# Second products of an MLP moved between attention scores, in row tiling

## The chip, the cores and the metric

The kernel runs on one core of a Trainium2 chip. The metric is the device time of one execution in microseconds. Most executions agree within 0.3%; times below are medians of several runs. A ratio between two kernels is the mean time of one kernel's fast runs over the mean of the other's of the same rounds, so it is not quite the ratio of the medians quoted beside it. Where two kernels are said to differ by so many us, that is the difference of their ratios, taken of 430 us.

## The reference

Attention with one extra unit in the softmax denominator, then an MLP with a squared ReLU:

```python
# q, k, v: (8, 12, 448, 64); w_in: 768 x 2048; w_out: 2048 x 768
scores = q @ k.T / sqrt(64);  e = exp(scores - m)
attn = e / (sum(e) + exp(-m) + 1e-9)
x = (attn @ v)                 # as 3584 tokens x 768
r = maximum(x @ w_in, 0)       # "first product"
out = (r * r) @ w_out          # "second product", float32
```

## The kernel before

The program is a loop over 54 units. A unit is a pair of heads of one batch (batch 0 is cut in two, so it has 12 units; from unit 12 on a unit covers all 448 queries). A unit computes its scores and exponentials, and row sums and values of the unit before it. After unit 53 one more pass does row sums and values alone; where a text speaks of the last unit, which has no scores, it means this pass. MLP work of earlier batches is poured in between, so that TensorE (the matrix engine) always has something to do while ScalarE exponentiates.

TensorE can be split into tiles. Scores contract over 64 numbers, so two of them run at once in two halves of the rows (row tiling). Values and row sums have 64 outputs, so two run at once in halves of the columns (column tiling). MLP products fill the array (full tiling), or are written as two column halves when they follow the values. All of them write the banks of PSUM, eight in this kernel, which the other engines then read ("evict"). In the code `drain` issues MLP matmuls; in the texts a drain is the pause of TensorE at a change of tiling.

```python
s_psum = ... bufs=2 (two banks each)   x_psum = ... bufs=1   m_psum = ... bufs=3   # 8 banks

def product(out_, lhsT, rhs, start, stop):
    if halved[0]:
        for x in (0, 64):
            nc.tensor.matmul(out_[x:x + 64], lhsT[:, x:x + 64], rhs, start=start, stop=stop)
    else:
        nc.tensor.matmul(out_, lhsT, rhs, start=start, stop=stop)

# the loop, shortened
    scores(u, et, 0)
    drain(share[0] * 0.45)             # MLP matmuls, full tiling
    scores(u, et, 1)
    rcp = row_sums(prev, pes)
    values(prev, pet, xp, 0); values(prev, pet, xp, 1)
    halved[0] = True
    drain(share[0] * 0.15)             # MLP matmuls, column halves
    for step in range(3):
        add_chunks(u, et, es, step)    # VectorE: three additions for the next row sums
        drain(share[0] * (0.15, 0.1, 0.15)[step])
    normalise(prev, xp, rcp)           # VectorE: values * reciprocal of row sums
```

A first-product tile is taken from PSUM by VectorE (relu, then square); a second-product tile by ScalarE (copy with a scale).

The softmax here doesn't subtract the row's maximum and nothing guards it: scores larger than these inputs give would overflow.

## Time and profile before

| | before |
|---|---|
| time, median of runs | 430.2 us |
| span of the profiled run | 430.7 us |
| TensorE, VectorE, ScalarE busy | 98%, 57%, 57% |
| chain of work that ended last (followed back from the last instruction), on TensorE | 92% |

The page gives busy time of each engine, but a busy TensorE is not one at its peak. What counts is the distance between starts of consecutive matmuls, compared with the columns that they stream. The prediction below reads that. One caution on this profile: the profiled execution itself took 432.5 us, 2 us over the median. Its clock records are at half rate from 11.6 to 18.4 us, which no later profile here has, and unit 13 starts at 47.04 us where the others have 44.8 to 45.6. So 2 us of its early part are chance.

### The profile page before, as it was taken

The page shows a single profiled execution, that of the slowest core. Times are in us where ns is not written, and L with a number is a line of the kernel's source. Part 1 is how long each engine was busy: PE and PEld are TensorE (multiplying, and loading weights), DVE is VectorE, ACT ScalarE, POOL GpSimd, SP SyncE. Part 2 cuts the span into 40 slices and gives each one's busy share as a digit, 9 for nine tenths or more (in the row PEclk, how much of TensorE's full clock was granted, in tenths as well). Part 3 has the DMA queues.
Part 4 walks back from the last instruction along what each step waited for, and adds up shares of the span by engine and source line. Part 5 has one row for each costly group of instructions (what it writes and reads, how often), then busy time and mean ns, then how long its engine had stood idle before and what let it go on. Part 6 is the DMA issues. An engine that isn't in the chain of part 4 may idle for free.

```text
span 430.7 us, 9136 instructions
## 1 busy us (share of the span) xinstructions
PE 421.4 (98%) x3975; PEld 248.1 (58%) x3975; DVE 246.6 (57%) x489; ACT 247.6 (57%) x359; POOL 33.2 (8%) x52
## 2 busy tenths in 40 slices
PE   8989899999999999999999999999999999999996
PEld 3557675554465666554556665654556666564454
DVE  4759695268822596348842488248762278428700
ACT  4698867764555756674456755774555655740011
POOL 7541100010000100010000100030000000000000
PEclk9699899999999999999999999999999999999999
DMA  9999999399312893259811697139902200010022
GB/s 200 197 197 204 209 218 180 96 156 210 58 39 75 146 215 63 74 83 214 128 37 52 99 223 127 39 61 207 192 3 75 74 3 2 37 54 22 0 75 74
DMA packets 79129, 47.56 MB, mean 110 GB/s; under 512 B 50672, under 2 KB 75120, under 8 KB 78704
## 3 DMA queue, kind: packets, MB, share of 16 engines
q0 software_dynamic: 24160, 22.17, 32.2%
q1 hardware_dynamic: 54208, 24.11, 25.5%
q10 hardware_dynamic: 720, 0.69, 0.6%
q8 instruction: 31, 0.51, 0.5%
q14 instruction: 10, 0.08, 0.1%
HBM read 45.71 MB, written 19.32 MB: 151 GB/s over the span
## 4 chain that ended last, share of the span: by engine, by line
PE 92%; DVE 2%; ACT 2%; DMA 2%; issue 1%; ACTq 0%
PE mp L254 37%; PE mp L252 31%; PE sp L187 9%; PE xp L223 8%; PE mp L231 3%; PE sp L175 2%; DMA kr<-in_k_dram 2%; ACT et L155 1%; PE mp L147 1%; PE mp L376 1%; DVE es L204 1%; DVE qk L150 0%; ACT rcp L233 0%; DVE xt L242 0%; DVE es L208 0%
## 5 line engine op out<-in xcount | busy, mean ns | idle before, releaser
L155 ACT ACTIVATE et<-sp 112x896 f16<-112x896 f32 (+2 forms) x192 | 165.9, 914 | 109.8 <-PE sp L187 92.1
L200 DVE TENSOR_TENSOR es<-et 112x896 f16<-112x896 f16 x84 | 51.6, 622 | 103.5 <-ACT et L155 103.4
L274 DVE TENSOR_SCALAR rt<-mp 128x512 f16<-128x512 f32 (+1 forms) x122 | 77.4, 635 | 35.3 <-PE mp L252 24.1
L254 PE MATMUL mp<-xt,win 128*128 128x512 f16 (+3 forms) x456 | 84.8, 339 | 0.0
L254 PE MATMUL mp<-wout,g 128*128 128x512 f16 (+1 forms) x471 | 82.3, 330 | 0.0
L252 PE MATMUL mp<-wout,g 128*64 128x256 f16 (+1 forms) x850 | 71.9, 322 | 0.0
L252 PE MATMUL mp<-xt,win 128*64 128x384 f16 (+3 forms) x816 | 71.2, 325 | 0.2 <-DVE xt L242 0.2
L254 PEld LDWEIGHTS <-g 128*128 128x128 f16 x471 | 44.3, 98 | 33.9 <-issue 2.5
L304 ACT ACTIVATE ot<-mp 128x512 f32<-128x512 f32 (+1 forms) x56 | 27.3, 487 | 63.4 <-PE mp L254 51.7
L254 PEld LDWEIGHTS <-win 128*128 128x128 f16 x456 | 41.6, 98 | 36.6 <-issue 2.1
L252 PEld LDWEIGHTS <-g 128*64 128x64 f16 x850 | 47.7, 110 | 19.4
L252 PEld LDWEIGHTS <-win 128*64 128x64 f16 x816 | 45.4, 110 | 22.6 <-issue 1.0
L276 DVE TENSOR_TENSOR g<-rt 128x512 f16<-128x512 f16 (+1 forms) x124 | 49.5, 399 | 6.5 <-ACT rt L272 2.3
L223 PE MATMUL xp<-et,vn 112*64 112x448 f16 (+2 forms) x432 | 46.5, 338 | 0.3 <-DVE xt L242 0.3
L187 PE MATMUL sp<-qk 64*112 64x224 f16 x576 | 42.8, 268 | 0.0
L187 PEld LDWEIGHTS <-qk 64*112 64x112 f16 x576 | 26.9, 128 | 25.4 <-issue 25.4
L233 ACT ACTIVATE rcp<-mp,one_b 128x448 f32<-128x448 f32 (+2 forms) x54 | 32.2, 597 | 3.1 <-PE mp L231 2.8
L242 DVE TENSOR_TENSOR xt<-xp,rcp 128x448 f16<-128x448 f32 (+2 forms) x54 | 30.6, 566 | 3.5 <-ACT rcp L234 3.5
L223 PEld LDWEIGHTS <-vn 112*64 112x64 f16 x432 | 24.8, 112 | 10.3 <-issue 0.6
L234 ACT ACTIVATE rcp<-rcp 128x448 f32<-128x448 f32 (+2 forms) x54 | 28.9, 535 | 1.7
L78 POOL DMA_DIRECT2D vn<-in_v_dram x10 | 9.0, 902 | 243.2 <-PE xp L223 229.1
L202 DVE TENSOR_TENSOR es<-es 112x896 f16<-112x896 f16 x42 | 26.1, 623 | 1.0
(36 smaller groups left out, 136.5 us busy)
## 6 DMA issues: line engine op xcount, KB each, us to landing
out_dram<-ot SPq DMA_DIRECT2D x11, 384.0 KB, 2.3
vn<-in_v_dram POOLq DMA_DIRECT2D x6, 672.0 KB, 9.1
stage_q<-in_q_dram POOLq DMA_DIRECT2D x5, 676.0 KB, 11.1
stage_k<-in_k_dram POOLq DMA_DIRECT2D x5, 676.0 KB, 14.0
win<-in_moe_w_in_dram POOLq DMA_DIRECT2D x8, 384.0 KB, 13.8
wout<-in_moe_w_out_dram POOLq DMA_DIRECT2D x4, 768.0 KB, 20.2
out_dram<-ot SPq DMA_DIRECT2D x8, 288.0 KB, 2.6
out_dram<-ot SPq DMA_DIRECT2D x8, 192.0 KB, 2.7
```

The costliest lines, as they stand in the source:

```text
L155: nc.scalar.activation(out=out_, in_=in_, func=AF.Exp, scale=scale)
L187: nc.tensor.matmul(sp[:, odd, h * (S // 2):(h + 1) * (S // 2)], qk[r, which, kx:kx + 2 * P - 1:2], qk[r, 0, x:x + S // 2], start=True, sto ...
L200: nc.vector.tensor_add(f[:, step], e[:, 2 * step], e[:, 2 * step + 1])
L223: nc.tensor.matmul(xp[64 * h:64 * h + 64, 0:n], vns[b][:, 2 * pr + h, kk, :], of_head(chunk(et, u, c, kk), u, h), start=(kk == 0), stop=(k ...
L233: nc.scalar.activation(out=rcp[:, 0:n], in_=zp[:, 0:n], func=AF.Ln, bias=one_b)
L234: nc.scalar.activation(out=rcp[:, 0:n], in_=rcp[:, 0:n], func=AF.Exp, scale=-1.0)
L242: nc.vector.tensor_mul(xts[b // 2][:, pr, c:c + n], xp[:, 0:n], rcp[:, 0:n])
L252: nc.tensor.matmul(out_[x:x + 64], lhsT[:, x:x + 64], rhs, start=start, stop=stop)
L254: nc.tensor.matmul(out_, lhsT, rhs, start=start, stop=stop)
L274: nc.vector.tensor_scalar(out=rt[:, 0:m], in0=hp[:, 0:m], scalar1=0.0, scalar2=None, op0=ALU.max)
L276: nc.vector.tensor_mul(g[:, 0:m], rt[:, 0:m], rt[:, 0:m])
L304: nc.scalar.activation(out=ot[:, n0:n1], in_=op[:, 0:n1 - n0], func=AF.Copy, scale=OUT_SCALE)
```

## The change

The intent is to save changes of tiling. Between a unit's two halves of scores, which run in row tiling, a second product now runs in row tiling too: the 2048 contracted numbers are taken as two halves of each block of 128, one per row tile, into two PSUM banks. ScalarE evicts the first bank and VectorE adds the second. After the values come first products, in column halves. Work is handed out in whole tiles, and second products of a batch wait one batch longer.

```diff
+    def tile_out(t0, ts, n0, n1):
+        ...
+        lo = m_psum.tile([128, 512], FP32, name="mp") if rows else None
+        for fb in range(NFFB):
+            g = gts[t0][fb][:, ts * 128:(ts + 1) * 128]
+            if rows:
+                for x, o in ((0, op), (64, lo)):
+                    nc.tensor.matmul(o[:, 0:w], g[x:x + 64], wout[x:x + 64, fb, n0:n1], ...)
+        ...
+        nc.scalar.activation(out=ot[:, n0:n1], in_=op[:, 0:w], func=AF.Copy, scale=OUT_SCALE)
+        if rows:
+            nc.vector.scalar_tensor_tensor(out=ot[:, n0:n1], in0=lo[:, 0:w], scalar=OUT_SCALE,
+                                           in1=ot[:, n0:n1], op0=ALU.mult, op1=ALU.add)
 ...
-             2 * NPAIR - 1: [(1, 128, 256), (2, 0, 128), (2, 128, 256)]}
+             2 * NPAIR - 1: [(1, 128, 256), (2, 0, 128)]}
+    last, t0 = (2, 128, 256), 384
 ...
-        ready[(b + 2) * NPAIR - 1] = [(1, t0, n), (2, t0, n)]
+        ready[(b + 2) * NPAIR - 1] = [(1, t0, n), last]      # second product of the batch before
+        last = (2, t0, n)
 ...
+    def later_batch(i, u, prev, xp, pet, pes):               # from unit 12 on
+        if u:
+            scores(u, et, 0)
+            if outs and i >= MIXED + 3:
+                mode[0] = ROWS2
+                budget -= run(outs)                          # one second-product tile, 512 or 256 wide
+            else: ...                                        # first products, full tiling
+            scores(u, et, 1)
+        rcp = row_sums(prev, pes)
+        values(...)
+        others = [three additions] if u else []
+        others.append(lambda: normalise(prev, xp, rcp))
+        mode[0] = COLS2
+        while True:
+            ...                                              # first products, or spare second ones
+            budget -= run(tiles)
+            if others:
+                others.pop(0)()
+        for o in others:
+            o()
```

More of the change, by code (lines that the diff above doesn't have):

```diff
@@ L242, in normalise @@
         nc.vector.tensor_mul(xts[b // 2][:, pr, c:c + n], xp[:, 0:n], rcp[:, 0:n])
-    gts = {}
-    halved = [False]
+    gts, ots = {}, {}
+    FULL, COLS2, ROWS2 = range(3)
+    mode = [FULL]
     def product(out_, lhsT, rhs, start, stop):
-        if halved[0]:
+        if mode[0] == COLS2:
             for x in (0, 64):
@@ L254, in product, with tile_in @@
             nc.tensor.matmul(out_, lhsT, rhs, start=start, stop=stop)
-    def mlp_in(t0, n):
-        gt = gts[t0] = []
+    def tile_in(t0, n, f0, per):
+        gt = gts.setdefault(t0, [])
         xt, x0 = xts[t0 // (2 * S)], t0 % (2 * S)
-        per = max(1, 512 // n) if n < 384 else 1
-        for f0 in range(0, NFFB, per):
-            hp = m_psum.tile([128, 512], FP32, name="mp")
-            for j in range(per):
-                fb = f0 + j
-                for dc in range(DCH):
-                    product(hp[:, j * n:(j + 1) * n], win[:, dc, fb * 128:(fb + 1) * 128],
-                            xt[:, dc, x0:x0 + n], start=(dc == 0), stop=(dc == DCH - 1))
-                    if j < per - 1 or dc < DCH - 1:
-                        yield n / 2.4
-            m = per * n
-            rt = r_pool.tile([128, 512], FP16, name="rt")
-            if t0 == 0 and f0 % 8 == 0:
-                nc.scalar.activation(out=rt[:, 0:m], in_=hp[:, 0:m], func=AF.Relu)
-            else:
-                nc.vector.tensor_scalar(out=rt[:, 0:m], in0=hp[:, 0:m], scalar1=0.0, scalar2=None, op0=ALU.max)
-            g = g_pool.tile([128, 512], FP16, name=f"g{f0}")
-            nc.vector.tensor_mul(g[:, 0:m], rt[:, 0:m], rt[:, 0:m])
-            for j in range(per):
-                gt.append(g[:, j * n:(j + 1) * n])
-            yield n / 2.4
+        hp = m_psum.tile([128, 512], FP32, name="mp")
+        for j in range(per):
+            fb = f0 + j
+            for dc in range(DCH):
+                product(hp[:, j * n:(j + 1) * n], win[:, dc, fb * 128:(fb + 1) * 128],
+                        xt[:, dc, x0:x0 + n], start=(dc == 0), stop=(dc == DCH - 1))
+                if j < per - 1 or dc < DCH - 1:
+                    yield n / 2.4
+        m = per * n
+        rt = r_pool.tile([128, 512], FP16, name="rt")
+        if t0 == 0 and f0 % 8 == 0:
+            nc.scalar.activation(out=rt[:, 0:m], in_=hp[:, 0:m], func=AF.Relu)
+        else:
+            nc.vector.tensor_scalar(out=rt[:, 0:m], in0=hp[:, 0:m], scalar1=0.0, scalar2=None, op0=ALU.max)
+        g = g_pool.tile([128, 512], FP16, name=f"g{f0}")
+        nc.vector.tensor_mul(g[:, 0:m], rt[:, 0:m], rt[:, 0:m])
+        for j in range(per):
+            gt.append(g[:, j * n:(j + 1) * n])
+        yield n / 2.4
     def store(c, ot, n0, n1):
@@ L291, in store @@
             c += m
-    def mlp_out(t0, n):
-        gt = gts.pop(t0)
-        for ts in range(n // 128):
-            ot = osb_pool.tile([128, DM], FP32, name="ot")
-            for n0, n1 in ((0, 512), (512, DM)):
-                op = m_psum.tile([128, 512], FP32, name="mp")
-                for fb in range(NFFB):
-                    product(op[:, 0:n1 - n0], gt[fb][:, ts * 128:(ts + 1) * 128], wout[:, fb, n0:n1],
-                            start=(fb == 0), stop=(fb == NFFB - 1))
-                    if fb < NFFB - 1:
-                        yield (n1 - n0) / 2.4
-                nc.scalar.activation(out=ot[:, n0:n1], in_=op[:, 0:n1 - n0], func=AF.Copy, scale=OUT_SCALE)
-                if n1 == DM or t0 + ts * 128 + 128 == NT:
-                    store(t0 + ts * 128, ot, 0 if n1 < DM or t0 + ts * 128 + 128 < NT else n0, n1)
-                if n1 < DM:
-                    yield (n1 - n0) / 2.4
-            yield (DM - 512) / 2.4
+    def tile_out(t0, ts, n0, n1):
+        w = n1 - n0
+        tok = t0 + ts * 128
+        if n0 == 0:
+            ots[tok] = osb_pool.tile([128, DM], FP32, name="ot")
+        ot = ots[tok]
+        op = m_psum.tile([128, 512], FP32, name="mp")
+        rows = mode[0] == ROWS2
+        lo = m_psum.tile([128, 512], FP32, name="mp") if rows else None
[3 more added lines that the diff above has]
+                for x, o in ((0, op), (64, lo)):
+                    nc.tensor.matmul(o[:, 0:w], g[x:x + 64], wout[x:x + 64, fb, n0:n1],
+                                     start=(fb == 0), stop=(fb == NFFB - 1))
+            else:
+                product(op[:, 0:w], g, wout[:, fb, n0:n1], start=(fb == 0), stop=(fb == NFFB - 1))
+            if fb < NFFB - 1:
+                yield w / 2.4
+        nc.scalar.activation(out=ot[:, n0:n1], in_=op[:, 0:w], func=AF.Copy, scale=OUT_SCALE)
+        if rows:
+            nc.vector.scalar_tensor_tensor(out=ot[:, n0:n1], in0=lo[:, 0:w], scalar=OUT_SCALE, in1=ot[:, n0:n1],
+                                           op0=ALU.mult, op1=ALU.add)
+        last = tok + 128 == NT
+        if n1 == DM or last:
+            store(tok, ot, n0 if last else 0, n1)
+        yield w / 2.4
     warm = consts.tile([128, 512], FP16)
@@ L336, with left, run @@
     load_v(1, 3, 6)
-    work, left = [], [0.0]
+    ins, outs, begun = [], [], []
     def queue(part, t0, n):
-        work.append((mlp_in if part == 1 else mlp_out)(t0, n))
-        left[0] += (NFFB * DCH * n if part == 1 else n // 128 * NFFB * DM) / 2.4
+        if part == 1:
+            per = max(1, 512 // n) if n < 384 else 1
+            for f0 in range(0, NFFB, per):
+                ins.append([per * DCH * n / 2.4, tile_in(t0, n, f0, per)])
+        else:
+            for ts in range(n // 128):
+                for n0, n1 in ((0, 512), (512, DM)):
+                    outs.append([NFFB * (n1 - n0) / 2.4, tile_out(t0, ts, n0, n1)])
+    def left():
+        return sum(t[0] for t in ins + outs)
+    def run(tiles):
+        ns, gen = tiles.pop(0)
+        for _ in gen:
+            pass
+        return ns
     def drain(ns):
-        while work and ns > 0:
-            got = next(work[0], None)
+        while ins and ns > 0:
+            got = next(ins[0][1], None)
             if got is None:
-                work.pop(0)
+                ins.pop(0)
             else:
                 ns -= got
-                left[0] -= got
+                ins[0][0] -= got
     FIRST = 192
@@ L357 @@
     NU = len(units)
-    ready = {NPAIR - 1: [(1, 0, 128)],
-             2 * NPAIR - 1: [(1, 128, 256), (2, 0, 128), (2, 128, 256)]}
-    t0 = 384
+    MIXED = 2 * NPAIR
+    ready = {NPAIR - 1: [(1, 0, 128)], 2 * NPAIR - 1: [(1, 128, 256), (2, 0, 128)]}
+    last, t0 = (2, 128, 256), 384
     for b in range(1, B):
         n = 384 if b % 2 == 0 else 512
-        ready[(b + 2) * NPAIR - 1] = [(1, t0, n), (2, t0, n)]
+        ready[(b + 2) * NPAIR - 1] = [(1, t0, n), last]
+        last = (2, t0, n)
         t0 += n
@@ L389, in take_up, with first_batch @@
                 queue(*part)
-            share[0] = left[0] / NPAIR
-    for i in range(NU + 1):
-        u = units[i] if i < NU else None
-        prev = units[i - 1] if i > 0 else None
-        xp = rcp = None
-        if prev:
-            pet, pes = et, es
-            xp = x_psum.tile([128, 512], FP32, name="xp")
-        if u:
-            b, pr = u[0:2]
-            if pr == 0 and 0 < b and b + 1 < B:
-                load_v(b + 1, 0, NPAIR)
-                stage(b + 1)
-            et = e_pool.tile([P, RUN * 2 * S], FP16, name="et")
-            es = e_pool.tile([P, 4 * S], FP16, name="es")
-            scores(u, et, 0)
-            if i == 0:
-                keep_warm(4)
-            elif i < NPAIR:
-                keep_warm(1)
-                scores(u, et, 1)
-            if i == NPAIR:
-                rcp = row_sums(prev, pes)
-                values(prev, pet, xp, 0)
-                values(prev, pet, xp, 1)
-                normalise(prev, xp, rcp)
-                take_up(i - 1)
-            if i in transpose_at:
-                transposes(*transpose_at[i])
-            if i in regroup_at and i < NPAIR:
-                regroup(*regroup_at[i])
-            drain(share[0] * (0.45 if i != NPAIR else 0.0))
-            if i == 0 or i >= NPAIR:
-                scores(u, et, 1)
+            share[0] = left() / NPAIR
+    def first_batch(i, u, prev, xp, pet, pes):
+        scores(u, et, 0)
+        if i == 0:
+            keep_warm(4)
+        elif i < NPAIR:
+            keep_warm(1)
+            scores(u, et, 1)
+        rcp = None
+        if i == NPAIR:
+            rcp = row_sums(prev, pes)
+            values(prev, pet, xp, 0)
+            values(prev, pet, xp, 1)
+            normalise(prev, xp, rcp)
+            take_up(i - 1)
+        if i in transpose_at:
+            transposes(*transpose_at[i])
+        if i in regroup_at and i < NPAIR:
+            regroup(*regroup_at[i])
+        if i > NPAIR:
+            drain(share[0] * 0.45)
+        if i == 0 or i >= NPAIR:
+            scores(u, et, 1)
         if prev and i != NPAIR:
@@ L432 @@
             regroup(*regroup_at[i])
-        halved[0] = u is not None
+        mode[0] = COLS2
         drain(share[0] * 0.15)
         for step in range(3):
-            if u:
-                add_chunks(u, et, es, step)
+            add_chunks(u, et, es, step)
             drain(share[0] * (0.15, 0.1, 0.15)[step])
-        halved[0] = False
+        mode[0] = FULL
         if prev and i != NPAIR:
             normalise(prev, xp, rcp)
+    def later_batch(i, u, prev, xp, pet, pes):
+        togo = NPAIR - (i - 1) % NPAIR
+        budget = left() / togo
+        if u:
+            scores(u, et, 0)
+            if i in transpose_at:
+                transposes(*transpose_at[i])
+            if outs and i >= MIXED + 3:
+                mode[0] = ROWS2
+                budget -= run(outs)
+                mode[0] = FULL
+            else:
+                ns = 0.0
+                while ins and ns < 1500.0 and ns + 0.5 * ins[0][0] < budget:
+                    ns += run(ins)
+                budget -= ns
+            scores(u, et, 1)
+        rcp = row_sums(prev, pes)
+        values(prev, pet, xp, 0)
+        values(prev, pet, xp, 1)
+        if i in regroup_at:
+            regroup(*regroup_at[i])
+        others = []
+        if u:
+            others += [lambda step=step: add_chunks(u, et, es, step) for step in range(3)]
+        others.append(lambda: normalise(prev, xp, rcp))
+        mode[0] = COLS2
+        while True:
+            tiles = outs if i >= MIXED + 3 and (len(outs) > togo - 1 or not ins) else ins
+            if not tiles or 0.5 * tiles[0][0] > budget:
+                break
+            budget -= run(tiles)
+            if others:
+                others.pop(0)()
+        mode[0] = FULL
+        for o in others:
+            o()
@@ new lines @@
+    for i in range(NU + 1):
+        u = units[i] if i < NU else None
+        prev = units[i - 1] if i > 0 else None
+        pet, pes = et, es
+        xp = x_psum.tile([128, 512], FP32, name="xp") if prev else None
+        if u:
+            b, pr = u[0:2]
+            if pr == 0 and 0 < b and b + 1 < B:
+                load_v(b + 1, 0, NPAIR)
+                stage(b + 1)
+            et = e_pool.tile([P, RUN * 2 * S], FP16, name="et")
+            es = e_pool.tile([P, 4 * S], FP16, name="es")
+        if i < MIXED:
+            first_batch(i, u, prev, xp, pet, pes)
+        else:
+            later_batch(i, u, prev, xp, pet, pes)
+        if i != NPAIR:
@@ L444 @@
             transposed_loads(b + 1)
-    drain(1e12)
+    queue(*last)
+    before = len(outs) - last[2] // 64
+    while ins or outs:
+        if outs and (not ins or before > 0 and before * NFFB >= len(ins) * 6):
+            run(outs)
+            before -= 1
+        else:
+            run(ins)
 _INS = ['q', 'k', 'v', 'moe_w_in', 'moe_w_out']
```

## The prediction

> **What bounds the kernel now.** I read the page first (busy shares, the chain that ended last), then the waits of TensorE, then TensorE's order of time in one steady pair, then the first 90 us, where transfers matter. The page says that TensorE is busy almost throughout, and that the chain that ended last runs through it for 92% of the span:
>
> ```profile
> PE 421.4 (98%) x3975; PEld 248.1 (58%) x3975; DVE 246.6 (57%) x489; ACT 247.6 (57%) x359; POOL 33.2 (8%) x52
> ...
> PE 92%; DVE 2%; ACT 2%; DMA 2%; issue 1%; ACTq 0%
> ```
>
> The waits view of TensorE lists seven waits, 5.8 us together; the two longest entries are below (total, times, longest), and all are in the first 50 us. So nothing in the steady part starves TensorE, and only what TensorE itself spends can be saved there.
>
> ```profile
> PE mp L231 <- DVE es L208: 2.2, 3, 1.0
> PE mp L376 <- DVE warm L313: 1.2, 1, 1.2
> ```
>
> Busy is not peak, though. In TensorE's order of time (start, duration, line), one pair is scores, 15 full products, scores, row sums, values, then products in column halves:
>
> ```profile
> 206.59 0.59 PE L187 MATMUL sp<-qk 64*112 64x224 f16 x8
> 207.12 3.41 PE L254 MATMUL mp<-xt,win 128*128 128x512 f16 x15
> 210.46 0.59 PE L187 MATMUL sp<-qk 64*112 64x224 f16 x8
> 210.98 0.38 PE L231 MATMUL mp<-es,ones 112*64 112x448 f16 x2
> 211.20 0.92 PE L223 MATMUL xp<-et,vn 112*64 112x448 f16 x8
> ```
>
> The reader is to look at distances of starts. Consecutive full products start 216 ns apart, but 15 of them take 210.46 - 207.12 = 3.34 us, 0.10 more than 15 x 0.216. Score matmuls run as two row tiles at once, a pair every 95 ns, yet four pairs take 0.53 us and not 0.38. The loss is at changes of tiling. I took the start of every matmul between 88 and 376 us and subtracted its streaming time (columns at 2.4 per ns). Inside one tiling the excess is 2 to 3 ns. At changes the medians are: row to full 98, first full product another 10; full to row 96, first row pair another 48; row to column 96 plus 26 at the first; column to row 99 plus 48. A pair has four changes, 252 ns for going to full and back, 269 ns for going to column and back.
>
> **What the Trainium skill says.** "TensorEngine Tiling (Array Packing)", section Key Properties: changing the tiling mode drains the TensorEngine, changing the tile does not. The trace agrees, with the 96 to 99 ns above. The same page, Gotcha 1, says that row tiles must write different PSUM banks; that is why the changed product takes two. The trace shows it for the scores, whose two row tiles write two banks and keep 95 ns per pair of 224 columns. "TensorE: Matmul & The Clock Gate", section "What's actually happening", says that an idle window of about 3.4 us halves TensorE's clock for at least such a window. This trace has clock records at half from 45.7 to 49.1 us, after waits of 0.72 and 0.41 us at 44 to 45 us, so a hole need not even be a whole window long.
>
> **The change part by part.**
> (1) Tiling. From unit 15 on (units counted in the program's loop, 54 in all), one second product, 512 or 256 columns wide, sits between the two score halves in row tiling. Row to full and back goes away: 252 ns. I worked the queue rule through by hand-count: 35 of units 15 to 53 get such a product; 17, 18, 23, 24 find no second product and use full first products. Two of the 35 (15, 16) lie in the early part, discussed under (4). 33 x 0.252 = 8.3 us saved. The change to column and back stays.
> (2) Streaming. A row-tiled product of 128x512 is two matmuls of 64 rows together, as a column-tiled one is two of 64 columns together. I take 216 ns per pair for 512 and 109 for 256, as in column and full tiling. The risk is the weights: two loads of 64x128 per pair. The scores do two loads of 64x112 per 95 ns; scaled to 128 columns, 109 ns (an estimate), which just fits the narrow products. So no change: 0 us. The tail of pure products grows, from 41 to 56.3 us of streaming, but that is the same work moved.
> (3) VectorE. Each of the 35 tiles needs a second eviction, fused multiply and add from the second bank. By the 128x512 eviction's 688 ns and 128x384's 553 ns I estimate 0.70 us for 512 and 0.45 for 256, some 20 us of VectorE, 247 to 267 us, 62%. It stays off the bound on average. What can bite is the ring of three mp banks: a row tile takes two, row sums the third. Steps on VectorE start this far apart:
>
> ```profile
> 297.32 0.69 DVE L274 TENSOR_SCALAR rt<-mp 128x512 f16<-128x512 f32 x1
> 298.04 0.43 DVE L276 TENSOR_TENSOR g<-rt 128x512 f16<-128x512 f16 x1
> 298.38 0.62 DVE L242 TENSOR_TENSOR xt<-xp,rcp 128x448 f16<-128x448 f32 x1
> 298.92 0.68 DVE L274 TENSOR_SCALAR rt<-mp 128x512 f16<-128x512 f32 x1
> ```
>
> so one first-product tile with an attention step beside it costs 0.72 + 0.34 + 0.54 = 1.60 us at 512 columns, some 1.40 at 384, against 1.30 and 0.97 on TensorE. In most units the ring absorbs it. Units 28, 40 and 52 run five 384-column tiles in a row, and the second bank of the next row tile then waits: the fourth relu ends at 1.1 + 3 x 1.40 + 0.55 = 5.85 us, TensorE arrives at 5 x 0.97 + 0.53 = 5.38. About 0.5 us, three times: 1.5 us lost.
> (4) The early part. The second products of tokens 128 to 383 (10.2 us of streaming) move from units 13 to 18 to units 19 to 24. Those six units then hold only 15.4 us of products instead of 25.6, and run faster than the next batch's inputs arrive:
>
> ```profile
> 64.35 3.71 SPq L130 DMA_TRANSPOSE qk<-stage_q  x1
> 68.10 6.76 SPq L130 DMA_TRANSPOSE qk<-stage_k  x2
> ```
>
> These transposed loads of q and k wait for staging copies, which queue behind the weights: the DMA engines are saturated from 48 us on, and the last transpose lands 5.1 us after its issue at 71.8, at 76.9 us. Nothing in the change moves that. Now:
>
> ```profile
> 82.44 0.59 PE L187 MATMUL sp<-qk 64*112 64x224 f16 x8
> 82.97 2.23 PE L254 MATMUL mp<-wout,g 128*128 128x512 f16 x13
> ...
> 87.71 0.59 PE L187 MATMUL sp<-qk 64*112 64x224 f16 x8
> ```
>
> Unit 18 begins at 82.44, 5.5 us after the data. Changed, unit 13 begins at 47.0 as before and units of about 4.8 to 5.4 us (2.56 of products and some 2.2 of attention; unit 13 also has transposes) bring TensorE to unit 18 at about 73 to 75 us, where it waits until 77.0. Unit 18 itself has 2.56 us of products and takes about 5, so unit 19 begins at 82.2. To break even it would have to begin at 87.71 - 10.24 = 77.5. Loss 4.7 us, and I add 0.8 for the clock, which the hole of 2 to 4 us may halve for one window. So 5.5 us lost; what units 15 and 16 save is swallowed by this wait.
> Sum: 430.2 - 8.3 + 1.5 + 5.5 = 428.9 us.
>
> **The rivals.**
> A: the wait for transfers doesn't form. If units 13 to 17 are slower than I think, they use up the same time, so little changes; if the loads land earlier, up to 5 us come back and the time is about 424. Against it: the DMA chain does not depend on TensorE after 47 us.
> B: row-tiled products do not stream at full pace, because of weight loads of 128 columns or because two banks accumulate at once. The scores speak against it, but they neither accumulate nor use 128 columns. If only the 256-wide ones slowed to twice their time, 17 tiles x 1.7 us would add 29 us: about 457, slower.
> C: the array drains between scores of 112 columns and products of 128 too. Then nothing is saved and the losses stand: about 437. The skill speaks of modes, and both need 64 rows and more than 64 columns; so I hold it unlikely.
> D: ScalarE or VectorE becomes the bound through the ring of three banks in more units than three. Per unit ScalarE needs about 4.4 us plus a copy and VectorE some 5 to 6, of about 8 us. Another 2 to 4 us at most: 431 to 433.
>
> **Range and chances.** The gain of 8.3 us is the firmest term, the 5.5 us of the early part is uncertain by 2, the ring by 1.5 and more upward than downward. 428.9, with 425.0 to 433.0 for 8 in 10. Two per cent is 8.6 us; faster by that would need the whole gain and no loss at all: 0.04. Slower by it needs B or C with losses: 0.05. Within: 0.91.
>
> **What the changed profile would show.** Right: no excess where row products meet scores, four score pairs after a row product starting 95 ns apart from the first; 216 and 109 ns per row pair; a TensorE wait on the transposed loads of batch 2 of 2 to 4 us at about 73 to 77 us, and unit 19 starting near 82; a tail without scores some 15 us longer; a few waits of about 0.5 us of row products for VectorE. Wrong: pairs of row products further apart than 216 or 109 ns; drains of 97 ns that stay; unit 18 starting well before 76 us; waits on mp in most units.

## More of the kernel before

`row_sums` of a unit reads what the three additions made. `values` writes the one bank of `x_psum`, which `normalise` of the unit before has to have read.

## The result

The changed kernel takes 440.5 us (438.4 to 441.6, six runs) against 430.3 us: a ratio of 1.023, 95% interval 1.021 to 1.025. It is slower. The prediction of 428.9 us with a range up to 433.0 was wrong.

The page of the changed kernel, busy shares and the chain that ended last:

```profile
PE 419.3 (96%) x4422; PEld 264.6 (60%) x4422; DVE 263.3 (60%) x524; ACT 244.4 (56%) x359; POOL 33.1 (8%) x52
...
PE 73%; DVE 12%; DMA 9%; ACT 3%; issue 1%; SPq 1%; POOL 0%; POOLq 0%
```

VectorE is no busier than estimated, 263 us. Yet the chain that ended last runs through it for 12% of the span, 2% before. It is late, not full. TensorE's waits (total, times, longest) are these, and unlike before they reach into the steady part:

```profile
PE mp L231 <- DVE es L202: 3.0, 3, 2.4
PE sp L175 <- ACT et L155: 2.6, 7, 0.7
PE sp L187 <- DMA qk<-stage_k: 1.9, 1, 1.9
PE xp L223 <- DVE xt L242: 1.8, 10, 0.5
```

This view counts only idle time after a matmul's modelled end, so it shows less than is lost. TensorE's order of time in one pair, with a 256-wide product between the scores, shows more:

```profile
201.08 0.59 PE L187 MATMUL sp<-qk 64*112 64x224 f16 x8
201.51 1.91 PE L306 MATMUL mp<-wout,g 64*128 64x256 f16 x32
203.26 0.55 PE L187 MATMUL sp<-qk 64*112 64x224 f16 x8
203.90 0.38 PE L231 MATMUL mp<-es,ones 112*64 112x448 f16 x2
204.43 0.95 PE L223 MATMUL xp<-et,vn 112*64 112x448 f16 x8 [0.15 <-DVE xt L242]
```

The first three rows are what the change wanted: eight scores, 16 pairs of product and eight scores follow each other with no drain, 1.75 us for 16 pairs of 256 columns, 109 ns each. But row sums start 0.64 us after the scores, and values 0.53 us after the row sums; before, it was 0.52 and 0.22. VectorE in the same stretch (L200 and L202 are the additions, L242 the normalisation, L274 and L276 relu and square):

```profile
201.50 0.68 DVE L274 TENSOR_SCALAR rt<-mp 128x512 f16<-128x512 f32 x1
202.22 0.43 DVE L276 TENSOR_TENSOR g<-rt 128x512 f16<-128x512 f16 x1
202.56 0.62 DVE L200 TENSOR_TENSOR es<-et 112x896 f16<-112x896 f16 x1
203.22 0.63 DVE L202 TENSOR_TENSOR es<-es 112x896 f16<-112x896 f16 x1
203.76 0.62 DVE L242 TENSOR_TENSOR xt<-xp,rcp 128x448 f16<-128x448 f32 x1
204.29 0.42 DVE L314 SCALAR_TENSOR_TENSOR ot<-mp,ot 128x256 f32<-128x256 f32 x1
```

The last addition ends at 203.85 and row sums start at 203.90; the normalisation ends at 204.38 and values start at 204.43. Both stand in VectorE's queue behind relu and square of a tile that TensorE finished only at the end of the unit before.

To see where time is lost I cut each trace at the start of unit 19 and of unit 53. For each stretch, counted from the first matmul at 1.2 us, I took its length less the pure streaming of its matmuls (columns at 2.4 per ns, half for each of two tiles that run at once). Streaming is 377.4 us in all in each kernel, so moved work cancels in this "excess":

| excess, us | to unit 19 | units 19 to 52 | unit 53 to end | span |
|---|---|---|---|---|
| before | 24.9 (22.9 without the chance 2 us) | 22.6 | 4.7 | 430.7 |
| changed | 29.6 | 20.7 | 9.8 | 438.7 |
| predicted difference | +5.5 | -6.8 | 0 | |
| measured difference | +6.7 | -1.9 | +5.1 | |

So the early part came out nearly as predicted, the steady part kept 1.9 of 6.8 us, and the end lost 5.1 us that the prediction did not have at all. The sum, +9.9, is the 10.2 us between the medians within their scatter.

### The profile page after: what moved, and what is told of

It is laid out like the page before. It is cut to its first block, busy times and chain, and to the rows that moved or that the text cites. A ratio compares the mean times of both kernels' runs of the same rounds, so it can differ in the third digit from the quotient of the medians.

```text
span 438.7 us, 10101 instructions
## 1 busy us (share of the span) xinstructions
PE 419.3 (96%) x4422; PEld 264.6 (60%) x4422; DVE 263.3 (60%) x524; ACT 244.4 (56%) x359; POOL 33.1 (8%) x52
## 4 chain that ended last, share of the span: by engine, by line
PE 73%; DVE 12%; DMA 9%; ACT 3%; issue 1%; SPq 1%; POOL 0%; POOLq 0%
PE mp L254 22%; PE mp L306 19%; PE mp L256 17%; PE xp L223 7%; PE sp L187 5%; DVE rt L274 4%; DMA kn<-in_k_dram 3%; DVE es L200 3%; DMA win<-in_moe_w_in_dram 3%; DVE g L276 3%; PE mp L231 2%; DMA vn<-in_v_dram 2%; ACT et L155 2%; DVE xt L242 1%; DMA qk<-stage_k 1%
## 5 line engine op out<-in xcount | busy, mean ns | idle before, releaser
L274 DVE TENSOR_SCALAR rt<-mp 128x512 f16<-128x512 f32 (+1 forms) x122 | 77.5, 635 | 79.5 <-PE mp L254 55.3
L254 PE MATMUL mp<-xt,win 128*64 128x384 f16 (+2 forms) x1216 | 114.2, 339 | 0.2 <-DVE xt L242 0.2
L306 PE MATMUL mp<-wout,g 64*128 64x512 f16 (+1 forms) x1120 | 104.2, 333 | 0.6 <-DVE rt L274 0.6
L254 PEld LDWEIGHTS <-win 128*64 128x64 f16 x1216 | 74.9, 110 | 32.5 <-issue 0.5
L306 PEld LDWEIGHTS <-g 64*128 64x128 f16 x1120 | 58.4, 94 | 35.5 <-issue 2.0
L200 DVE TENSOR_TENSOR es<-et 112x896 f16<-112x896 f16 x84 | 51.8, 619 | 3.9 <-ACT et L155 3.8
L276 DVE TENSOR_TENSOR g<-rt 128x512 f16<-128x512 f16 (+1 forms) x124 | 49.5, 399 | 4.6 <-ACT rt L272 0.4
L314 DVE SCALAR_TENSOR_TENSOR ot<-mp,ot 128x512 f32<-128x512 f32 (+1 forms) x35 | 20.3, 581 | 48.6 <-ACT ot L312 48.6
L256 PE MATMUL mp<-xt,win 128*128 128x512 f16 (+2 forms) x256 | 44.1, 329 | 0.0
L187 PEld LDWEIGHTS <-qk 64*112 64x112 f16 x576 | 30.6, 128 | 19.5 <-issue 14.1
L256 PE MATMUL mp<-wout,g 128*128 128x512 f16 (+1 forms) x224 | 37.5, 326 | 0.0
L256 PEld LDWEIGHTS <-win 128*128 128x128 f16 x256 | 24.5, 103 | 16.4 <-issue 0.9
L242 DVE TENSOR_TENSOR xt<-xp,rcp 128x448 f16<-128x448 f32 (+2 forms) x54 | 30.6, 566 | 3.0 <-PE xp L223 1.9
L256 PEld LDWEIGHTS <-g 128*128 128x128 f16 x224 | 21.8, 98 | 15.4 <-issue 0.3
L202 DVE TENSOR_TENSOR es<-es 112x896 f16<-112x896 f16 x42 | 26.1, 622 | 0.8
## 6 DMA issues: line engine op xcount, KB each, us to landing
stage_q<-in_q_dram POOLq DMA_DIRECT2D x5, 676.0 KB, 10.2
```

Source lines behind the costliest of these rows:

```text
L187: nc.tensor.matmul(sp[:, odd, h * (S // 2):(h + 1) * (S // 2)], qk[r, which, kx:kx + 2 * P - 1:2], qk[r, 0, x:x + S // 2], start=True, sto ...
L200: nc.vector.tensor_add(f[:, step], e[:, 2 * step], e[:, 2 * step + 1])
L242: nc.vector.tensor_mul(xts[b // 2][:, pr, c:c + n], xp[:, 0:n], rcp[:, 0:n])
L274: nc.vector.tensor_scalar(out=rt[:, 0:m], in0=hp[:, 0:m], scalar1=0.0, scalar2=None, op0=ALU.max)
L276: nc.vector.tensor_mul(g[:, 0:m], rt[:, 0:m], rt[:, 0:m])
L306: nc.tensor.matmul(o[:, 0:w], g[x:x + 64], wout[x:x + 64, fb, n0:n1], start=(fb == 0), stop=(fb == NFFB - 1))
```

## The experiments

Theory A: VectorE's order is the cause. Additions and normalisation stand last in a unit, and the next unit's row sums and values now come too soon for them. Rival B: the second eviction loads VectorE too much. Rival C: row tiling itself is slower than thought. The early part, the prediction's fourth step, is a separate question. (These letters are not those of the prediction's rivals.) Ten kernels were run, all correct but one.

### E1: additions ahead of the tiles

```diff
-            budget -= run(tiles)
             if others:
                 others.pop(0)()
+            budget -= run(tiles)
```

> Correct results. Each attention step of VectorE (three additions, then the normalisation) is put ahead of the product tile it used to follow. Theory A (VectorE does the additions and the normalisation last, and with a 256-wide product between the scores the next pair's row sums and values come too soon for them): the waits of row sums and values shrink from about 10 us to about 2, time about 431 (430 to 433). Rival B (the second eviction loads VectorE) and rival C (row tiling itself is slow): nothing of the load or of the tiling changes, so about 440 (439 to 441).

Measured: 433.7 us, ratio to before 1.0076 (1.0058 to 1.0094), where the changed kernel has 1.023. That is 6.6 us back with the same instructions in another order. The excess of units 19 to 52 fell from 20.7 to 15.7. Taken unit by unit, all of this lies in the 13 units that have a 256-wide product between their scores (0.2 to 0.5 us each). The same pair in TensorE's order of time:

```profile
199.29 1.91 PE L306 MATMUL mp<-wout,g 64*128 64x256 f16 x32
201.04 0.55 PE L187 MATMUL sp<-qk 64*112 64x224 f16 x8
201.52 0.38 PE L231 MATMUL mp<-es,ones 112*64 112x448 f16 x2
201.73 0.92 PE L223 MATMUL xp<-et,vn 112*64 112x448 f16 x8
```

Row sums start 0.48 us after the scores, values 0.21 after the row sums: both waits are gone. A holds for 5.0 us of the steady part. The time missed its upper bound of 433 by 0.7 us: 2.4 us of waits stayed in the last unit (E8).

### E2: no second eviction

```diff
-        if rows:
-            nc.vector.scalar_tensor_tensor(out=ot[:, n0:n1], in0=lo[:, 0:w], ...)
```

> Wrong results on purpose: the second bank of a row-tiled product is never read, so 35 VectorE evictions (20.3 us busy) go. Theory A: they mostly run where VectorE would wait for TensorE anyway, so at most 1 to 2 us, about 439. Rival B (load of VectorE): most of the 8 us of new waits in the steady part goes, about 432.

Measured: 441.6 us, 1.0239 (1.0207 to 1.0271), results wrong. Removing 20 us of VectorE work (its busy time fell from 263 to 244 us) gained nothing, the excess of units 19 to 52 stays at 20.7, and the wait of values for the normalisation is the same line as in the changed kernel:

```profile
PE xp L223 <- DVE xt L242: 1.8, 10, 0.5
```

B falls. The changed kernel's VectorE rows above show why: the second eviction (L314) stands after the normalisation, where VectorE next waits for TensorE anyway.

### E3: the same order, product in full tiling

```diff
-                mode[0] = ROWS2
                 budget -= run(outs)
```

> Correct results. The order of the changed kernel, but the product between the scores in full tiling, one bank, one eviction. Theory A and the prediction's first step (two drains saved in each of 33 to 35 pairs, 0.25 us each): about 8 us slower than the changed kernel less the waits that the longer gap hides, 445 to 448. Rival C (row tiling costs more than it saves): faster than the changed kernel, 430 to 438.

Measured: 443.4 us, 1.0292 (1.0270 to 1.0314). Neither range that I gave was met. Row tiling is faster, by 0.6% or 2.7 us, so C falls, but the gain is far less than 8 us. Part of what the two drains cost is time in which VectorE catches up: with full tiling the excess of the steady part is 24.3 and not 20.7, only 3.6 apart. In six units with a 256-wide product (32, 34, 36, 44, 46 and 48) it is the same in both kernels within 0.01 us, 0.9 us each. And E3 shows that the new order alone, without row tiling, is 12.6 us slower than the kernel before.

### E4: second product of tokens 128 to 383 queued as before

```diff
-             2 * NPAIR - 1: [(1, 128, 256), (2, 0, 128)]}
-    last, t0 = (2, 128, 256), 384
+             2 * NPAIR - 1: [(1, 128, 256), (2, 0, 128), (2, 128, 256)]}
+    last, t0 = None, 384
# and a second product is taken only when its first product is complete
```

> Correct results. The second product of tokens 128 to 383 is queued with the first, as in the kernel before, and no longer one batch later; row tiling and all else kept. Prediction's fourth step (the early pairs outrun the transposed loads of batch 2, 4.7 us lost by the start of unit 19): 4 to 5 us faster than the changed kernel, 435 to 437, and the wait of TensorE for those loads gone. Rival: the early part costs nothing and all 10 us are in the steady part: 440.

Measured: 433.7 us, 1.0071 (1.0056 to 1.0086), 6.8 us faster than the changed kernel. The early excess fell from 29.6 to 22.4. Unit 18 of the changed kernel, in TensorE's order of time:

```profile
73.49 0.30 PE L187 MATMUL sp<-qk 64*112 64x224 f16 x1
75.69 0.59 PE L187 MATMUL sp<-qk 64*112 64x224 f16 x7 [1.90 <-DMA qk<-stage_k]
76.21 4.46 PE L256 MATMUL mp<-xt,win 128*128 128x256 f16 x24
80.61 0.59 PE L187 MATMUL sp<-qk 64*112 64x224 f16 x8
```

It begins at 73.49, waits 2.2 us for the transposed loads, and then runs its 24 products in 4.40 us where unit 14 needs 2.72. Clock records are at half from 76.3 to 79.7 us. With E4 unit 18 finds its data there and has second products to run:

```profile
81.43 0.59 PE L187 MATMUL sp<-qk 64*112 64x224 f16 x8
81.86 1.91 PE L306 MATMUL mp<-wout,g 64*128 64x256 f16 x32
83.61 0.60 PE L187 MATMUL sp<-qk 64*112 64x224 f16 x8
```

The gain beat my 4 to 5 us. With the wait gone, what row tiling saves in units 15 to 18 counts, the clock is not halved there, and TensorE's waits for exponentials (`sp <- ACT et` at L175) fall from 2.6 to 1.4 us; how the gain divides among these was not tested apart. E4 also leaves units 19 to 24 without second products, so the short gaps of units 20 and 22 are gone.

### E5 and E6: E1 and E4 together, and the same in full tiling

> Correct results. E1 and E4 together: additions ahead of tiles, and the early second product queued early. If the lateness of VectorE (A) and the outrun transposed loads (prediction's fourth step) are separate causes, their gains add: 440.5 - 7 - 7 = 427 us (425 to 428.5), faster than the kernel before. If they are one cause seen twice, about 433.

Measured: 429.6 us, 0.9954 (0.9920 to 0.9989). The gains add but for about 1.6 us, and the time is 1 us above the range I gave. Of the 1.6 us, 1.1 is explained: units 20 and 22, in which E1 won 0.53 and 0.54 us, have no narrow product between the scores in E4, so the new order has nothing to win there.

> Correct results. E5 with the product between the scores in full tiling. With most waits gone, this shows what row tiling is worth by itself. Prediction's first step (0.25 us in some 33 to 35 pairs): 8 us slower than E5, about 435. If the drains saved are mostly given back to waits whatever the order: 2 to 4 us slower than E5, as E3 is of the changed kernel.

Measured: 434.6 us, 1.0082 (1.0057 to 1.0108), 5.5 us slower than E5. Neither number I gave. The pair in E6, then in E5:

```profile
203.70 0.59 PE L187 MATMUL sp<-qk 64*112 64x224 f16 x8
204.23 3.63 PE L256 MATMUL mp<-wout,g 128*128 128x512 f16 x16
207.79 0.59 PE L187 MATMUL sp<-qk 64*112 64x224 f16 x8
208.31 0.38 PE L231 MATMUL mp<-es,ones 112*64 112x448 f16 x2
```

```profile
201.21 0.59 PE L187 MATMUL sp<-qk 64*112 64x224 f16 x8
201.64 3.62 PE L306 MATMUL mp<-wout,g 64*128 64x512 f16 x32
205.09 0.55 PE L187 MATMUL sp<-qk 64*112 64x224 f16 x8
205.57 0.38 PE L231 MATMUL mp<-es,ones 112*64 112x448 f16 x2
```

From first scores to row sums it is 4.61 us in full tiling and 4.36 in row tiling: 0.25 us, the prediction's figure for two drains. In units 19 to 52 there are 28 such pairs in E5, 7.0 us. Two of them (units 29 and 41) lose 0.57 us each at the ring of three banks (next paragraph), and two more (31 and 43), whose second bank comes late too, 0.14 each; full tiling with its single bank does not lose this 1.4 us. 7.0 less 1.4 is 5.6, and the excess of these units differs by 5.5 (22.9 against 17.4).

The ring shows after the five tiles of units 28, 40 and 52 of the changed kernel, as predicted: that is, in units 29, 41 and 53. In its order of time the 512-wide product starts one matmul and then waits for a relu to empty its second bank:

```profile
155.04 5.07 PE L254 MATMUL mp<-xt,win 128*64 128x384 f16 x60
160.04 0.59 PE L187 MATMUL sp<-qk 64*112 64x224 f16 x8
160.47 0.38 PE L306 MATMUL mp<-wout,g 64*128 64x512 f16 x1
161.05 3.61 PE L306 MATMUL mp<-wout,g 64*128 64x512 f16 x31 [0.20 <-DVE rt L274]
```

### E7: second products cut evenly

```diff
-                for n0, n1 in ((0, 512), (512, DM)):
+                for n0, n1 in ((0, DM // 2), (DM // 2, DM)):
```

> Correct results. The changed kernel with the second product cut into two of 384 columns in place of 512 and 256; order of VectorE untouched. Theory A: the short gap between the scores, 1.75 us, becomes 2.6 us in every pair, so the waits of row sums and values after a 256-wide product (some 4 us in all) go: 436 to 437. If the width of the product has no part in it: 440.

Measured: 434.2 us, 1.0079 (1.0045 to 1.0113), 6.5 us faster than the changed kernel and 2 us better than I gave. VectorE's order is untouched; the shortest gap between the scores grew from 1.75 to 2.6 us. The excess of units 19 to 52 fell by 5.8 us, of which 1.1 lies in the four units that lost at the ring (29, 31, 41, 43) and the rest in the units that had a 256-wide product: no row product of this trace waits for the ring any more, which I had not counted. This says from another side what E1 says: VectorE was late by a few tenths of a microsecond, against the shortest gap.

### E8 to E10: the last unit, and the even cut on top

```diff
             scores(u, et, 1)
+        else:                      # the last unit has no scores
+            budget -= run(outs)
+            budget -= run(ins)
         rcp = row_sums(prev, pes)
```

> Correct results. The changed kernel with one edit: the last unit runs a second-product and a first-product tile ahead of its row sums. In the changed kernel's trace the last unit loses 2.6 us waiting for additions, 0.3 for the normalisation, and then runs at half clock from 369.8 to 373.2 us, 1.6 us more in two groups: 4.5 us. If these are on the path, 4 to 4.5 us faster than the changed kernel, about 436. If the waiting only moves into the tail: 440.

E9 is the changed kernel with this edit alone: 436.8 us, 1.0141 (1.0121 to 1.0161), 3.8 us faster than the changed kernel. Its excess from unit 53 on is 5.6 and not 9.8. The changed kernel's last unit in TensorE's order of time shows what it removes:

```profile
369.56 0.38 PE L231 MATMUL mp<-es,ones 112*64 112x448 f16 x2 [2.43 <-DVE es L202]
370.09 1.71 PE L223 MATMUL xp<-et,vn 112*64 112x448 f16 x8 [0.15 <-DVE xt L242]
371.54 2.78 PE L254 MATMUL mp<-wout,g 128*64 128x256 f16 x32
```

Row sums wait 2.4 us for the additions of the unit before, because there is no scoring in between. The clock records then are at half from 369.8 to 373.2 us, and eight values take 1.45 us instead of 0.76.

> Correct results. E5, and the last unit, which has no scores, runs one second-product tile and one first-product tile ahead of its row sums. In E1 its row sums waited 1.24 us and its values 1.21 us for VectorE. If that wait is on the path: 2 us faster than E5, about 425 (1.2% under the kernel before). If those tiles only move: the same as E5.

E8 puts the edit on E5: 425.7 us, 0.9883 (0.9857 to 0.9908), 3 us faster than E5. This beats the kernel before by 1.2%. E5's profile has half clock from 359.3 to 362.7 us, in this last pass, and E8's has none, so the gain includes what that cost.

> Correct results. E8 with second products of 384 and 384 columns. In E8's trace some 2 us of waits are left, most after the narrow product and in the three pairs with five tiles after the values. With the even cut these should go: 424 (422.5 to 425.5), 1.5% under the kernel before. If the ring of three banks bites with even tiles instead (each pair now has three or four tiles after the values): the same as E8 or 1 us slower.

E10, with the even cut as well: 426.2 us, 0.9889 (0.9871 to 0.9908). No more is won. The excess of units 19 to 52 is 17.2 against 17.4. The ring waits are gone, but row sums after eight of the units wait 0.14 us each, by the start times, so the even cut trades one small wait for another. E8 and E10 are equal within their intervals. The 424 us that I expected did not come; the other case that I gave did.

The excess of all kernels that were timed, E2 apart, in the stretches of the table above. The first and last columns also hold half clock, which differs from profile to profile: near unit 18, 6.8 us in E7 and E9, 3.4 in the changed kernel, E1 and E3, none in the others; near 45 us, 3.4 in the changed kernel and E9 alone; after unit 53, 3.4 in the changed kernel, E3, E4 and E5, none before the last matmul in the others. The middle column has none, so it is the one to compare:

| excess, us | to unit 19 | units 19 to 52 | unit 53 to end | span |
|---|---|---|---|---|
| E1 additions first | 29.3 | 15.7 | 7.7 | 431.3 |
| E3 full tiling | 29.6 | 24.3 | 9.3 | 441.8 |
| E4 early second product | 22.4 | 21.4 | 9.9 | 432.3 |
| E5 = E1 + E4 | 22.3 | 17.4 | 9.4 | 427.8 |
| E6 = E5 in full tiling | 23.1 | 22.9 | 7.4 | 432.0 |
| E7 even cut | 31.2 | 14.9 | 8.0 | 432.6 |
| E8 = E5 + last unit | 22.1 | 17.4 | 5.5 | 423.7 |
| E9 last unit alone | 31.1 | 20.7 | 5.6 | 436.0 |
| E10 = E8 + even cut | 22.0 | 17.2 | 5.4 | 423.3 |

## Why the prediction was wrong

What bounds the kernel before, and **step 1**, the tiling, were right. The drains vanish where row products meet scores (3 ns over streaming, in the median of 30 such changes each way, against 96 to 99 ns before), and each such pair is 0.25 us shorter where nothing else waits (E5 against E6). **Step 2** was right: 109 ns per pair of 256 columns, and row products are not slower (E3).

**Step 3**, VectorE, is the step that failed. Its busy time was right, 263 against the 267 us foretold, and so were the three waits at the ring, after the very units named (0.57 us each, where I had 0.5). But the step looked for lateness only at the ring of three banks: "In most units the ring absorbs it." Row sums need the additions and values need the bank that the normalisation empties, and these steps stand last in VectorE's queue. With the 256-wide product the time from a unit's start to its row sums is short. (There are 14 such products; rival B of the prediction counted 17.) The term was 1.5 us. In the steady part it cost 5.0 us more, shown by E1, which only reorders. It also leaves out the last unit, which has no scores and so no gap at all: 5.1 us in the trace, some 2.9 of them waits for VectorE and 1.6 the half clock that followed, of which E9 brings back 3.8 us in the timed runs. E1's steady part and E9 together are 8.8 of the 11.6 us between 428.9 and 440.5; the early part adds 1.2.

**Step 4**, the early part, was right in kind and close in size. I put unit 19 at 82.2 us, or 83.0 with the 0.8 for the clock, and it began at 82.20. That this is so near is partly luck, since two errors offset each other: the data came 1.3 us earlier than I said, and the half clock cost 1.7 us and not 0.8. Measured against an ordinary start of the kernel before it is 6.7 us, where I had 5.5; E4 gets it back.

**The rivals.** The prediction's D, an engine that becomes the bound through waits in more than three units, is nearest to what happened, but I gave it 2 to 4 us and the ring as its place. Its B and C, slow row products and drains that stay, did not occur. My chance of 0.05 for slower by over 2% had all its weight on those two.

## What to carry to other kernels

When you shorten a gap, list every consumer that stood behind it and the whole queue of the engine that feeds each one, not only the buffers; check the shortest gap of the schedule and its last round, not the mean. An engine at 60% can still be late, and then moving its urgent steps ahead in its queue, at no cost, gave 6.6 us here where removing 20 us of its work gave nothing. A saving of this kind is worth keeping once the waits are dealt with: E8 is 1.2% faster than the kernel before.

## What the Trainium skill lacked or had wrong

- "TensorEngine Tiling (Array Packing)", Key Properties, says that a mode change drains the engine but gives no size. Here it is 96 to 100 ns at each change, plus 48 ns for the first pair in row tiling, 26 for the first in column tiling and 10 for the first in full tiling.
- The same section does not say outright whether tiles of 64 rows with 112 and with 128 columns share a mode. They do: 3 ns over streaming where scores meet products.
- "TensorE: Matmul & The Clock Gate", "What's actually happening", puts the throttle after an idle window of about 3.4 us, and does not say there how much of it has to be idle. Here waits of 2.2 and 2.4 us were followed by half clock for 3.4 us each (76.3 to 79.7 and 369.8 to 373.2 us), though matmuls ran in the rest of the 3.4 us before; so a window need not be wholly idle.
- The same page, "LDWEIGHTS (loading the stationary operand)", gives columns over 1.2 in ns, some 107 ns for 128 columns. In the changed kernel a load of 64x128 takes 94 ns (mean of 1120) and one of 128x128 98 to 103 ns. "The mechanism" on that page lets a load run beside matmuls whose row group differs, and gives no number for two loads: here two loads of 64x128, started 1 to 2 ns apart, fit in each 109 ns of row-tiled products.
- No page that I read warns that an engine of moderate share can be late through the order of its queue; here 5.0 us, in 13 of 34 units, at 60% busy.
